# A convolution stage and a gated MLP on one core: absolute values, weight splits and a spectrum product moved between engines, and a new instruction order

## The chip, the cores and the metric

The kernel runs on one core of a Trainium2 chip. The metric is the device time of one execution in microseconds. The core's engines are named as in the profile: PE (TensorE, matmuls; PEld is its weight load), DVE (VectorE), ACT (ScalarE), POOL (GpSimd) and SP (SyncE, which issues most DMAs). Each engine works through its own list of instructions in order; semaphores between them carry the dependencies.

## The reference

A state-space convolution (S4D), and behind it a gated MLP (gMLP), each on a layer-normalized input and with a residual. L = 2048 positions, D = 512 channels, 128 states, all in float32.

```python
def A(u):                                   # S4D, as a long convolution
    dt = exp(log_dt)
    A = -exp(log_A_real) + 1j * A_imag;  C = (C_real + 1j * C_imag) * dt[:, None]
    P = exp((A * dt[:, None])[:, :, None] * arange(L))
    K = 2.0 * einsum("dn,dnl->dl", C, P).real
    y = irfft(rfft(u.T, 2 * L) * rfft(K, 2 * L))[..., :L].T
    return y + u * D_skip
def B(x):                                   # gMLP
    z = gelu(x @ w_in);  z1, z2 = z[..., :896], layernorm(z[..., 896:])
    g = einsum("ts,bsf->btf", w_sp, z2) + b_sp[None, :, None]
    return (z1 * g) @ w_out
h = x + A(layernorm(x));  out = h + B(layernorm(h))
```

## The kernel before, in words

**First phase (`phase_a`): the convolution as a Fourier transform by matmuls.** The channels are split in four stages, c = 0 to 3. Before the stages come the parameters (`params`, three calls: stage 0, stage 1, stages 2 and 3 together; absolute values and phases of C, phase increments split in a high and a low half, written to a stack in memory and loaded back as `sw`), the step sizes (`exp_exact`, a polynomial on 4 columns), tables of decays (`table`) and the layer norm of the input (`norm_x`, statistics on DVE, scaling on ACT and POOL).

The kernel K is built in 32 units of 16 channels (`unit`), eight to a stage. A unit's phases are two matmuls (`ps<-c_k,sw`); ACT takes sines and absolute values, POOL builds three decay tiles by products (`wa<-mt`) and weights one factor (`wb<-wb,wa`), DVE forms the factors (`f<-...`, `wa<-ps,wa`), and two groups of small matmuls (`ps<-f`, `ps<-wa,wb`) give `ks`. Then, by pieces:

- `piece_a` and `piece_c`, first step of the transform of the input and of K: 64x64 matmuls (`ps<-wb,...`).
- `piece_b`, second step for the input: 128x128 matmuls with 128 columns (`ps<-trio,a`, `ps<-big,a`), and `exchange`, a DMA that swaps halves of the spectrum between partitions.
- `piece_d`, second step for K (`ps<-big,a`), and at once the product with the input's spectrum in `trio` by DVE (`trio<-ps,trio`, 1024 elements). In stages 0 to 2 it works on the whole stage: eight groups of four matmul calls with 128 columns. In stage 3 it works in two halves of the channels: twice four groups of eight calls with 64 columns. Each call is two instructions in the trace.
- `piece_e`, the inverse transform (`ps<-c_inv,trio`), eight groups of 16 instructions a stage, copied to `big` by ACT or DVE.

All these calls are first recorded and then issued in an order written out by hand: `RANKS` gives every recorded call its place, `FORMS` chooses between two engines where the code offers two (`nc.either`), `BANKS` gives each result its PSUM bank. As all are issued from one helper, all have line L251. PSUM has five such banks here (three of double width).

**Between the phases.** Calls behind the last use of the units' buffers (the list is cut there) are issued by `rest`, inside the next phase, after that phase's loads (`xq`, `g`, `w1r`) have been put on SP's queue. After each of the last four copies of stage 3's `piece_e`, `rest` issues one quarter of the split of `w1` into a high and a low part (`split`: ACT casts, L688, and DVE subtracts, L689).

**Second phase (`phase_b1`).** `lines` finishes the inverse transform for a quarter n of the positions (`y<-big,g`, L754, four PSUM tiles), `add` adds the input, `moments` takes statistics (L780), `centre` and `root` the norm; `put_by` lets ACT copy a quarter's lines out of PSUM to a `stash` (L766), so that `add` later reads the stash (L771). For n = 0, `add` reads PSUM (L776) directly. The ACT table load for the next function (L893) stands ahead of the first lines. `column` is the first MLP product (`pz`, L880). Then follow the second half of that product (L982), the large product with `w_sp` (L1187) and the output (L1110).

Of the kernel before, what the change touches and what calls it, by code (L numbers as in the profile page):

```python
# [16 lines left out]
P = 128  # L17
# [20 lines left out]
    "0I000F0g1r0O0i0o0p1H1L1n1o0w2l1M2Z2L0805040302010607090A0B0C0D0E0G0H0K0N0R0T0Q0V0Y0X0J0x0y0z1E1G1T0L0U0S0a0k0l2i0+100-1B"  # L38
    "1F1J1P1Q1S1X1Y1d1q1y1t1u1v1w1z2J1611171h242P0M1W0c0Z0P1s0f180e270s2g2O2N1g0n0j1+2Q4a5F0h1l2A2Y3N121a0v0b1C0d1U0W14130r0t"
    "1f0m0q0u191A1Z151D1I1O1b1N1V1e1R1j1K1c1i252628292E2h2H2I2R2U2a2d2k2n2p2s2u2x2+312-3q3c3r373U3332393p363G3z3a383B3e3A644D"  # L40
    "3s4x453y443Q4u4J3f3b4X3H734K6t4L2F3O2w222T3S302K2f1x213F2y3C2V3I2C233J2B2r2m3P3E3W3R343M3L2e3K2o3X3Y3g3h3l3+3m3v3w3x3-41"
    "474A4E4G4Q4R4V4b4p514q525d5P4e726P6v4y5E4i6q4+5s534s6T5t4v4h5q4d4c6A5L4n546k624f4g5I4t5w7l7C768W8d1k1m2G2X2t3d3u481p1-20"
    "2D2M2bBd2j2q2z3Z3n3o494H4U4W4k4o5Q5u4O4P696B6C6D3T42434S6d6n4N4-675v6G6H6o6-775J5o5c6F6L6MHm6e6f6g6h6y6z70797A7B7I7J9K9f"
    "8UAY969UAZC3AdEk9c9-A0AlBBBGClFJFK6J6K6Q6R5N5O686E5S5V5y5-6N6O5k5r6m6u6p6w82837r7s7j7q7X7Z7a7b7V7W84852v3D3j4F4T4j4B4I4m"
    "4l564r575T6+7d7e2W2c2S353V3i3k3t46404Y4C4Z506I8T8b5G5H5K5U5W5X5Y5Z5a5b5n5j60666i7x7z4M4z5B4w5859555A5D5C5e5R5h5m8n9B9I7t"
    "7w7P7Y7c7k8E6S656X6U6V6W6Y6Z6a6b6s6c6x717+9F9L5M5l5i5x5z615f5g5+5p6j636l6r8B8e8f7T7m7g7R7S7U7Q7f7n7o7y7p87888Z97987L7O8A"
    "7K7M7N7u7v868C8J8D8S8i8s9495999x819C9R9Z9o898G787D7G7H8o8t8M8N7h7i74757E7F8w9DAqAr8u939k9l9J9YACAU9s9tAsAt9uABAMAc9N9jA8"
    "AG9g9nATAX9e9m9M9WBPBQCdCpCICQBiC8C9CABfBgCMCUCGCHCeE08H8X8O7-808F8K8Q8I8a8Y8P8j8k8r8vA9AgAh8L8g8m8R8V8c8q8l8y8p91909S92"
    "9a9b9+A+B09O8x9A8h8z8+9E8-9T9P9G9H9V9QA2A3B7BNBO9X9w9p9d9h9i9v9zA1ADA59qA6AEAFAPAQAmApBzBrBqBTBUBwBx9rAHAK9yA4A7ARAAAIAO"
    "AJANAVASAeAfCRDfDgAWAoALAaAbAiAyAnAjA-AuAkB6BABCBJBjDNDOB4AvBDB1B2B3BRBKBHBnBIBEBkBSBoC5D7DKDMBLBMBYB5BVBXBsBWBhBpBeBlBm"  # L50
    "BtBuC4CgD0D1CwCVDcBvCrDpDvAwAzAxB8B9BFBbBcC7BZBaCWCECOCFCXCYCbCZCkE5C+C-DWEHEIDUDtDSDeDDDPD5DEDXDZE2EAE8EGEpEtD+ECDzE3Dy"
    "E1EqEyD-EBEMEVETEZFtFuFZFbGTGaGIGbFAFLFpFvFkFlGSGVGUHGCBByC1B-C0CJCSCDCNCaCKCLCcCTCtCvEJFRFUCPC6CCB+C2CiCoCfCmD2CnCjCyCq"
    "D3DBDaF4F5CsD9D8ChCuCxCzDJD6DdDHDGDhDIDlDsFqH5HADLDRDAD4DCDFDVDjDQDkDTDYDiDbDnDxEXFSFTELEsDmFXDoFcFdDwENESEREYEgErEjElF0"
    "EiEhE-EvF9FDF-GhGoE4DrDqDuE6E9EUE7EDEKEEEFEcEWEmEnF7GNGcFYFPFGE+FEFVFsFFFiFjFeFrFyG1G2G6G7GgGnF2EzF6EwExF8FQFMFBFNFIFHFa"
    "FWFgFhG+G-H2FOF1HSHVFCHjHtEQEaEeEOEPEbEfEoFoEdEuF3FzG3GBF+GJGCGiGjGOGPHFHHI6I7GrGsGuGvHuHvHUHfHOHbHLHMHQHaHpHqHkHlHnHoHi"
    "H-HrHsHZHgHYHeIUIWIkIlIOIQIPIXIoIrIIIJImInILIMIpJPGWG5G4GDGEGFGeGQGXGYGRGdGyGfH6HBHzJFJGFxFwFnFfFmG0G9G8GAGGGLGKGZGMGlGm"
    "IyIzJ7GkHCHIH7HDHJHWHcHTHdHRHKHhHXHxHyIqJHJIGHGxGtGpGqGwH0H3H1H4GzH8H9HEHNHPItIuI-I3IKI1I4I5I9IbINIFIvIRIAIYIwIxJ1JaJcJd"
# [97 lines left out]
def exp_exact(nc, al, x, n):  # L155

    k, z, p = al(n), al(n), al(n)
    nc.vector.tensor_scalar(x, x, -87.0, 88.0, op0=ALU.max, op1=ALU.min)
# [7 lines left out]
    for i in range(7, 0, -1):
        nc.vector.scalar_tensor_tensor(p, p, co[i], z, op0=ALU.add, op1=ALU.mult)
    nc.vector.tensor_scalar(k.bitcast(I32), k, 127.0, 8388608.0, op0=ALU.add, op1=ALU.mult)
    nc.vector.scalar_tensor_tensor(x, p, 1.0, k, op0=ALU.add, op1=ALU.mult)
    return x  # L170
# [516 lines left out]
def split(nc, hi, lo, src):  # L687
    nc.scalar.copy(hi, src)  # L688
    nc.vector.tensor_sub(lo, src, hi.bitcast(F32))  # L689
# [8 lines left out]
def phase_b1(tc, es, right, left, rest, c_mean, mhalf, qt, ins, cst, wp, scr):  # L698
# [69 lines left out]
    def add(n, g):  # L768
        v = xqs[n % 3][:, 4 * g:4 * g + 4, :]
        if n:  # L770
            nc.vector.tensor_add(v, stash[n][:, g].rearrange("p (l x) -> p l x", l=4), v)  # L771
        else:
            h, y = g % 2, ys[n, g].rearrange("p l (x d) -> p l d x", d=4)
            v = xqs[n % 3][:, 4 * (g - h):4 * (g - h) + 8].rearrange("p l (d x) -> p l d x", d=4)[64 * h:64 * h + 64]
            for odd in range(2):
                nc.vector.tensor_add(v[:, odd::2], y[64 * odd:64 * odd + 64], v[:, odd::2])  # L776
# [523 lines left out]
```

## Time and profile before

| | |
|---|---|
| median of 3 runs | 854.41 us (850.94 to 854.44) |
| the profiled execution | 856.65 us; its span, first to last instruction, 854.9 us |
| granted PE clock, mean over the span | 0.972 of full speed |
| PE busy | 790.9 us (93%) |
| DVE, ACT, POOL busy | 612.4, 448.8, 286.7 us |

In the profile's rows, "128x64 f32 x16 [1.03 <-DVE big L251]" is 16 instructions on 128 partitions and 64 columns, ahead of which the engine was idle for 1.03 us until DVE's write to `big`. "Issue" is waiting for which the profile shows no cause. Durations of neighbours on one engine overlap slightly, since an instruction begins before the last one's end is noted. PE's granted clock is a share of full speed; where the clock is low, busy time is long time.

### The profile page before, as it was taken

Reading aid. Unit: us, or ns where it says so; the run is one execution under the profiler, and the core shown is the slowest. Engines: PE = TensorE matmul, PEld = TensorE weight load, DVE = VectorE, ACT = ScalarE, POOL = GpSimd, SP = SyncE. Lnnn points to the kernel's source line nnn. Section 1 sums busy time; section 2 is a strip of 40 time slices with the busy share of each in tenths; the row PEclk is TensorE's granted clock in tenths of the full one; section 3 lists DMA queues with packets and bytes.
Section 4 is the critical chain, followed back from the end, with each engine's and each line's share of the span. In section 5 each row is a group of like instructions: output and inputs, shape, how many; then the busy total and the mean of one; then the engine's idle time right before and its main releaser. Section 6 shows DMA issues by size and latency. Waiting matters only on the chain.

```text
span 854.9 us, 20107 instructions
## 1 busy us (share of the span) xinstructions
PE 790.9 (93%) x8145; PEld 674.4 (79%) x8145; DVE 612.4 (72%) x1176; ACT 448.8 (52%) x796; POOL 286.7 (34%) x340
## 2 busy tenths in 40 slices
PE   1569999999989877999999999999999999999998
PEld 0347789888978876788899988888888888888887
DVE  8999987777851357864357679988966985788533
ACT  6979988886740037555323255456534533354111
POOL 6969999976550000000032100224222002232200
PEclk9979999999995699999999999999999999999999
DMA  8504522525048113655246034899989547799632
GB/s 273 175 2 139 133 61 55 122 57 111 6 105 328 50 51 97 163 147 185 88 109 148 16 109 124 189 211 214 220 197 203 184 137 185 161 241 246 164 108 77
DMA packets 65005, 119.49 MB, mean 140 GB/s; under 512 B 6801, under 2 KB 21265, under 8 KB 63633
## 3 DMA queue, kind: packets, MB, share of 16 engines
q1 hardware_dynamic: 53248, 96.71, 38.2%
q0 software_dynamic: 11664, 21.50, 15.1%
q8 instruction: 64, 1.05, 0.5%
q14 instruction: 29, 0.23, 0.1%
HBM read 90.40 MB, written 19.40 MB: 128 GB/s over the span
## 4 chain that ended last, share of the span: by engine, by line
PE 84%; DVE 8%; ACT 5%; issue 2%; DMA 1%; SPq 0%; ACTq 0%; DVEq 0%
PE m L1187 33%; PE ps L251 25%; PE pz L982 9%; PE pz L880 7%; PE po L1110 7%; PE pl L1110 2%; DVE trio L251 2%; ACT big L251 2%; DVE f L251 1%; DVE ps L251 1%; DVE big L251 1%; DVE stats L780 1%; ACT ps L251 1%; DVE wa L251 1%; PE y L754 1%
## 5 line engine op out<-in xcount | busy, mean ns | idle before, releaser
L1187 PE MATMUL m<-wts,zc_wa 128*128 128x512 f32 x700 | 221.0, 395 | 0.0
L1187 PEld LDWEIGHTS m<-wts,zc_wa 128*128 128x128 f32 x700 | 131.7, 188 | 30.9
L1187 PE MATMUL m<-wts,zc_wb 128*128 128x512 f32 x350 | 138.0, 394 | 0.0
L1058 POOL DMA_DIRECT2D raws<-in_w_sp_dram x64 | 58.0, 995 | 214.7 <-DMA raws<-in_w_sp_dram 214.1
L251 POOL TENSOR_TENSOR wa<-mt 128x512 f32<-128x512 f32 x96 | 106.5, 1129 | 25.7 <-PE ps L251 19.8
L688 ACT CAST wts<-raws 128x512 fp32r<-128x512 f32 x112 | 69.1, 620 | 55.4 <-DMA raws<-in_w_sp_dram 25.7
L689 DVE TENSOR_TENSOR wts<-raws,wts 128x512 fp32r<-128x512 f32 x112 | 76.5, 685 | 17.0 <-ACT wts L688 16.9
L1187 PEld LDWEIGHTS m<-wts,zc_wb 128*128 128x128 f32 x350 | 65.8, 188 | 15.6
L251 PE MATMUL ps<-big,a 128*128 128x128 f32 (+1 forms) x512 | 74.6, 311 | 3.1 <-DVE big L251 1.0
L982 PE MATMUL pz<-w,ht 128*128 128x448 f32 x384 | 77.0, 362 | 0.0
L880 PE MATMUL pz<-ht,w1h 128*128 128x512 f32 (+1 forms) x248 | 73.8, 377 | 2.6 <-ACT ht L837 2.2
L251 PEld LDWEIGHTS ps<-big,a 128*128 128x128 f32 x512 | 71.0, 222 | 6.4 <-issue 1.3
L982 PEld LDWEIGHTS pz<-w,ht 128*128 128x128 f32 x384 | 72.0, 187 | 4.9
L988 POOL TENSOR_SCALAR sm<-sm 128x1 f32<-128x1 f32 x16 | 5.5, 344 | 209.3 <-DVE sm L987 209.3
L251 PE MATMUL ps<-c_inv,trio 128*128 128x128 f32 x512 | 65.6, 291 | 5.8 <-DVE big L251 3.2
L251 PEld LDWEIGHTS ps<-c_inv,trio 128*128 128x128 f32 x512 | 63.1, 205 | 7.4 <-DVE big L251 3.4
L1110 PE MATMUL po<-w,gz 128*128 128x512 f32 x252 | 61.7, 392 | 0.0
L251 DVE TENSOR_TENSOR trio<-ps,trio 128x1024 f32<-128x1024 f32 (+1 forms) x34 | 38.5, 1162 | 31.2 <-PE ps L251 27.5
L688 ACT CAST zc_wa<-raws 128x384 fp32r<-128x384 f32 (+1 forms) x70 | 36.9, 532 | 42.8 <-DVE raws L1092 22.4
L251 ACT COPY big<-ps 128x512 f32<-128x512 f32 x49 | 28.1, 588 | 58.1 <-PE ps L251 57.7
L1110 PEld LDWEIGHTS po<-w,gz 128*128 128x128 f32 x252 | 47.3, 188 | 10.7
L251 DVE TENSOR_TENSOR f<-ps,wa 128x512 f32<-128x512 f32 (+1 forms) x64 | 47.0, 750 | 11.7 <-ACT ps L251 9.8
(168 smaller groups left out, 1461.3 us busy)
## 6 DMA issues: line engine op xcount, KB each, us to landing
raws<-in_w_sp_dram SPq DMA_DIRECT2D x112, 256.0 KB, 4.1
raws<-in_w_sp_dram POOLq DMA_DIRECT2D x80, 256.0 KB, 5.9
trio<-trio SPq DMA_DIRECT2D x32, 256.0 KB, 4.4
scr_z<-zo SPq DMA_DIRECT2D x28, 256.0 KB, 2.1
big<-in_u_a_dram SPq DMA_DIRECT2D x8, 512.0 KB, 6.1
xq<-in_u_b_dram SPq DMA_DIRECT2D x4, 1024.0 KB, 8.8
g<-in_c_g_dram SPq DMA_DIRECT2D x4, 1024.0 KB, 7.7
scr_h<-xq SPq DMA_DIRECT2D x16, 256.0 KB, 4.3
```

The source lines that it names most:

```text
L251: r = getattr(getattr(self.nc, e), method)(*map(self.real, args), **{k: self.real(x) for k, x in kw.items()})
L688: nc.scalar.copy(hi, src)
L689: nc.vector.tensor_sub(lo, src, hi.bitcast(F32))
L754: nc.tensor.matmul(ys[n, g][o:o + 64, i, :], gs[n][w, l, r], qv[w, r, 16 * n + l], start=(r == 0), stop=(r == 1), tile_position=(64 * h, o))
L780: nc.vector.bn_stats(stats[:, n % 2, i, :], xqs[n % 3][:, i, :])
L880: nc.tensor.matmul(pt[:, w], a[:, q, f], ht[n][k][:, q, w], start=((q, i) == terms[0]), stop=((q, i) == terms[-1]))
L982: nc.tensor.matmul(pt[:, :FQ], a[:, q], w2[:, b, q, f], start=(q == 0 and i == 0), stop=(q == 3 and i == 2))
L988: nc.gpsimd.tensor_scalar_add(sm[:, 14:15], sm[:, 13:14], 1e-5)
L1058: nc.gpsimd.dma_start(r, ws[1], accum_op=ALU.add)
L1110: nc.tensor.matmul(pt, gz[fb][x][:, P * a:P * a + P], wo[:, y, fb, w], start=(first and fb == fbs[0] and i == 0), stop=(last and fb == fbs ...
L1187: nc.tensor.matmul(pt, x[:, f], y, start=(k == 0 and i == 0), stop=(k == KT - 1 and i == 2))
```

## The change

1. The parameters' six absolute values (`b` and `a` of three `params` calls) are ACT's `Abs` where DVE computed max(-x, x) of a tile in SBUF.
2. `exp_exact` keeps three of its tiles in PSUM, with one more instruction; the four `sw` memsets, the products `co`, `si`, the low halves and the weighting `wt` of the later units, which were DVE's or POOL's by `FORMS`, are POOL's.
3. `piece_d` of stage 3 is whole, as in the other stages. For its groups 1, 3 and 5 ACT copies the PSUM tile to SBUF and POOL does the product, in two instructions of 512 elements.
4. The four subtractions of the `w1` split are POOL's, and are issued after the second to fifth copies of stage 3's `piece_e` (by rank).
5. The first lines (n = 0) go through `put_by` and a stash too, like the others; the table load stands behind the copies of n = 0 and n = 1.
6. `RANKS`, `FORMS` and `BANKS` are new. The recorded calls go from 392 to 377 on DVE, 323 to 333 on ACT, 223 to 235 on POOL; PE keeps 280 groups and SP 70.

Read out by rank, PE's groups from unit 30's phases on are (U is a unit, with its two products; C, D, E the pieces of stage 3; `l` and `h` the halves):

```
before: U30 phases, U31 prod0, prod1, C0, C2, Dl3, C5, C7, U30 prod0, prod1, Dl2, C4, C6,
        Dh0, Dh3, Dh1, Dh2, Dl0, Dl1, E6, E7, E5, E2, E0, E4, E1, E3
after:  U30 phases, C2, U31 prod0, prod1, C5, U30 prod0, C0, U30 prod1, C6, C7, C4,
        D1, D4, D3, D2, D5, D7, D0, D6, E4, E1, E3, E6, E2, E5, E7, E0
```

DVE's products of Dl3, Dl2 and Dl0 stand behind E5 before. The last two exchange issues stand on either side of U30's phases before, and both ahead of them after. At the start, POOL has 13 instructions ahead of the last low half of the first stack before, and 18 after.

```diff
-def exp_exact(nc, al, x, n):
-    k, z, p = al(n), al(n), al(n)
+def exp_exact(nc, al, ps, x, n):
+    w, k, z, i = (al(n) for _ in range(4))
+    y, r, p = ps
...
-            nc.either(lambda: nc.vector.memset(sws[h][o:o + 32], 1.0), lambda: nc.gpsimd.memset(sws[h][o:o + 32], 1.0))
-    nc.vector.tensor_copy(dts, ldt)
-    exp_exact(nc, pm0, dts, NCH)
+            nc.gpsimd.memset(sws[h][o:o + 32], 1.0)
+    b = bank("dt", [P, 3, NCH])
+    e = exp_exact(nc, pm0, [b[:, i] for i in range(3)], ldt, NCH)
...
-        nc.vector.scalar_tensor_tensor(b, ci, -1.0, ci, op0=ALU.mult, op1=ALU.max)
+        nc.scalar.activation(b, ci, AF.Abs)
...
-        nc.vector.scalar_tensor_tensor(a, cr, -1.0, cr, op0=ALU.mult, op1=ALU.max)
+        nc.scalar.activation(a, cr, AF.Abs)
...
-            nc.either(lambda: nc.vector.tensor_sub(x, x, hi),
-                      lambda: nc.gpsimd.tensor_tensor(x, x, hi, op=ALU.subtract))
+            nc.gpsimd.tensor_tensor(x, x, hi, op=ALU.subtract)
...
-            nc.either(lambda: nc.gpsimd.tensor_tensor(wt, wt, mv[:, 2], op=ALU.mult), lambda: nc.vector.tensor_mul(wt, wt, mv[:, 2]))
+            nc.gpsimd.tensor_tensor(wt, wt, mv[:, 2], op=ALU.mult)
...
-    def piece_d(c, g, lo, n):
-        kn = 1 << (P // n).bit_length() - 1
-        pt = bank("s2", [P, 2 * n, 2 * kn])
+    def piece_d(c, g):
+        pt = bank("s2", [P, 64, 8])
         with nc.group():
-            for j in range(kn):
...
+            for j in range(4):
...
-        nc.vector.tensor_mul(v, pt.unsqueeze(1).to_broadcast([P, 2, 2 * n, 2 * kn]), v)
+        if c + 1 == NCH and g in (1, 3, 5):
+            t = trio[:, 0, 512 * (g // 2):512 * (g // 2) + 512].rearrange("p (x m) -> p x m", m=8)
+            nc.scalar.copy(t, pt)
+            for i in range(2):
+                nc.gpsimd.tensor_tensor(v[:, i], t, v[:, i], op=ALU.mult)
+        else:
+            nc.vector.tensor_mul(v, pt.unsqueeze(1).to_broadcast([P, 2, 64, 8]), v)
...
-        for lo, n in ((0, 32),) if c + 1 < NCH else ((0, 16), (16, 16)):
-            for g in range(n // 4):
-                piece_d(c, g, lo, n)
+        for g in range(8):
+            piece_d(c, g)
...
+        then = sorted(last, key=lambda o: o["rank"])[1:5]
...
-                if o in last:
+                if o in then:
                     next(between)
...
-def split(nc, hi, lo, src):
+def split(nc, hi, lo, src, engine=None):
     nc.scalar.copy(hi, src)
-    nc.vector.tensor_sub(lo, src, hi.bitcast(F32))
+    (engine or nc.vector).tensor_tensor(lo, src, hi.bitcast(F32), op=ALU.subtract)
...
-    rest(split(nc, w1h[:, q], w1l[:, q], w1r[:, q]) for q in range(4))
+    rest(split(nc, w1h[:, q], w1l[:, q], w1r[:, q], nc.gpsimd) for q in range(4))
...
-    stash = {n: hp.tile(...) for n, t in ((1, "h20"), (2, "h30"), (3, "h31"))}
+    stash = {n: hp.tile(...) for n, t in ((0, "h10"), (1, "h20"), (2, "h30"), (3, "h31"))}
...
-        nc.scalar.activation(stats[:, 1, 0, 0:1], mhalf, AF.Gelu_apprx_tanh)
         for n in range(2):
             for g in range(0, 4, 2):
                 lines(n, g, g + 1)
-        for g in range(0, 4, 2):
-            for f in add, moments:
-                f(0, g)
-                f(0, g + 1)
+        for n in range(2):
+            for g in range(4):
+                put_by(n, g)
+        nc.scalar.activation(stats[:, 1, 0, 0:1], mhalf, AF.Gelu_apprx_tanh)
         for g in range(4):
-            put_by(1, g)
+            add(0, g)
+            moments(0, g)
         centre(0)
```

More of the change, by code (lines that the diff above doesn't have):

```diff
@@ L37 @@
 RANKS = (
[L38 to L57, printed above, removed]
@@ L69 @@
-    "30023400301040213320243121044330112"
+    "414220313014444030432220022044434342124120412142014001422000123112321121011031223434430243400423134324420430131103321432"
+    "034214411300222000123324434132420203334344321432242224410132113203001432002102101211314313432104023143234243141003422442"
+    "030104322301034014314303413333144024"
 )
@@ L152, in rsqrt @@
     return y
-def exp_exact(nc, al, x, n):
-    k, z, p = al(n), al(n), al(n)
-    nc.vector.tensor_scalar(x, x, -87.0, 88.0, op0=ALU.max, op1=ALU.min)
-    nc.vector.tensor_scalar(k, x, 1.0 / math.log(2.0), MAGIC, op0=ALU.mult, op1=ALU.add)
-    nc.vector.tensor_scalar(k, k, MAGIC, None, op0=ALU.subtract)
+def exp_exact(nc, al, ps, x, n):
+    w, k, z, i = (al(n) for _ in range(4))
+    y, r, p = ps
+    nc.vector.tensor_scalar(y, x, -87.0, 88.0, op0=ALU.max, op1=ALU.min)
+    nc.vector.tensor_scalar(k, y, 1.0 / math.log(2.0), MAGIC, op0=ALU.mult, op1=ALU.add)
+    nc.vector.tensor_scalar(r, k, MAGIC, None, op0=ALU.subtract)
+    nc.vector.tensor_copy(w, y)
     hi = 0.693359375
-    nc.vector.scalar_tensor_tensor(z, k, -hi, x, op0=ALU.mult, op1=ALU.add)
-    nc.vector.scalar_tensor_tensor(z, k, hi - math.log(2.0), z, op0=ALU.mult, op1=ALU.add)
+    nc.vector.scalar_tensor_tensor(z, r, -hi, w, op0=ALU.mult, op1=ALU.add)
+    nc.vector.scalar_tensor_tensor(z, r, hi - math.log(2.0), z, op0=ALU.mult, op1=ALU.add)
     co = [1.0 / math.factorial(i) for i in range(9)]
     nc.vector.tensor_scalar_mul(p, z, co[8])
[L166 to L170, printed above, removed]
+    for d in range(7, 0, -1):
+        nc.vector.scalar_tensor_tensor(p, p, co[d], z, op0=ALU.add, op1=ALU.mult)
+    nc.vector.tensor_scalar(i.bitcast(I32), r, 127.0, 8388608.0, op0=ALU.add, op1=ALU.mult)
+    nc.vector.scalar_tensor_tensor(p, p, 1.0, i, op0=ALU.add, op1=ALU.mult)
+    return p
 class Late:
@@ L460, in params @@
                 nc.sync.dma_start(stk_d[c0 + c, h].rearrange("r p n -> p r n"), st6[64 * h:64 * h + 64, :, c, :])
-        times(co, co, mx, ALU.mult)
-        times(si, si, mn, ALU.mult)
-        times(co, co, si, ALU.add)
+        nc.gpsimd.tensor_tensor(co, co, mx, op=ALU.mult)
+        nc.gpsimd.tensor_tensor(si, si, mn, op=ALU.mult)
+        nc.gpsimd.tensor_tensor(co, co, si, op=ALU.add)
         for c in range(n):
@@ L621, in piece_e @@
         e = evac(o, pt.rearrange("p d r -> p r d"))
-        if c + 1 == NCH and s >= 4:
+        if c + 1 == NCH:
             last.append(e)
@@ L759, in phase_b1 @@
         load_g(n)
-    stash = {n: hp.tile([P, 4, 512], F32, tag=t, name=f"stash{n}") for n, t in ((1, "h20"), (2, "h30"), (3, "h31"))}
+    stash = {n: hp.tile([P, 4, 512], F32, tag=t, name=f"stash{n}") for n, t in ((0, "h10"), (1, "h20"), (2, "h30"), (3, "h31"))}
     def put_by(n, g):
@@ L769, in add @@
         v = xqs[n % 3][:, 4 * g:4 * g + 4, :]
[L770 to L776, printed above, removed]
+        nc.vector.tensor_add(v, stash[n][:, g].rearrange("p (l x) -> p l x", l=4), v)
     def moments(n, g):
```

44 lines of the change are left out of this document (30 added, 14 removed).

## Prediction

> **What bounds the kernel now.** I read the page's totals, then the busy time by stretches of the span (columns: PE, PEld, DVE, ACT, POOL busy us and instructions, granted clock, DMA share, GB/s), then PE's timeline where that table shows loss.
>
> ```profile
> span 854.9 us, 20107 instructions
> PE 790.9 (93%) x8145; PEld 674.4 (79%) x8145; DVE 612.4 (72%) x1176; ACT 448.8 (52%) x796; POOL 286.7 (34%) x340
> PEclk9979999999995699999999999999999999999999
> ...
> 0.00:40.00 40.00, 11.91 (x57) 7.22 (x61) 37.44 (x153) 31.43 (x70) 31.31 (x43) 1.00 0.73 239
> 40.00:60.00 20.00, 14.08 (x348) 9.88 (x340) 18.97 (x21) 14.93 (x34) 13.35 (x15) 0.74 0.01 3
> 60.00:240.00 180.00, 173.16 (x4196) 154.65 (x4187) 144.87 (x196) 151.46 (x216) 148.94 (x158) 1.00 0.34 81
> 240.00:265.00 25.00, 19.75 (x491) 17.93 (x490) 10.08 (x14) 9.99 (x18) 9.66 (x15) 0.86 0.76 228
> 265.00:286.00 21.00, 20.75 (x97) 20.75 (x98) 4.90 (x4) 0.19 (x1) 0.00 (x0) 0.50 0.42 169
> 286.00:313.00 27.00, 19.69 (x135) 19.15 (x139) 9.88 (x11) 6.38 (x10) 0.00 (x0) 0.82 0.15 44
> 313.00:345.00 32.00, 25.60 (x592) 23.89 (x587) 25.12 (x76) 21.32 (x39) 0.00 (x0) 1.00 0.41 109
> 345.00:855.00 510.00, 505.96 (x2265) 420.92 (x2265) 361.18 (x705) 213.09 (x414) 83.44 (x112) 1.00 0.64 159
> ```
>
> PE is the bound from 60 to 240 us (173.16 of 180) and from 345 us on (505.96 of 510). The diff touches nothing behind 345 us, so what is won ahead of it comes off the end one for one. Ahead of it lie three losses: the first 60 us, where DVE is the full engine (37.44 of 40 and 18.97 of 20); the last stage, 240 to 313 us; and the first lines, 313 to 345 us. The last stage hides its loss from the busy share: from 265 to 286 us PE is busy 20.75 of 21.00, at a granted clock of 0.50. PE's timeline there:
>
> ```profile
> 227.54 1.05 PE L251 MATMUL ps<-big,a 128*128 128x128 f32 x8
> ...
> 238.95 5.62 PE L251 MATMUL ps<-c_inv,trio 128*128 128x128 f32 x48
> ...
> 246.36 0.73 PE L251 MATMUL ps<-c_k,sw 128*128 128x512 f32 x2
> ...
> 251.73 1.97 PE L251 MATMUL ps<-big,a 128*128 128x64 f32 x16 [1.03 <-DVE big L251]
> ...
> 254.72 0.32 PE L251 MATMUL ps<-f 128*32 128x64 f32 x8
> 257.65 0.54 PE L251 MATMUL ps<-f 128*32 128x64 f32 x24 [2.60 <-issue]
> ...
> 258.95 3.68 PE L251 MATMUL ps<-big,a 128*128 128x64 f32 x16
> ...
> 265.25 20.75 PE L251 MATMUL ps<-big,a 128*128 128x64 f32 x96 [0.70 <-ACT big L251]
> 285.79 7.02 PE L251 MATMUL ps<-c_inv,trio 128*128 128x128 f32 x48
> 295.37 7.25 PE L251 MATMUL ps<-c_inv,trio 128*128 128x128 f32 x48 [2.56 <-DVE trio L251]
> 305.87 5.46 PE L251 MATMUL ps<-c_inv,trio 128*128 128x128 f32 x32 [3.24 <-DVE big L251]
> 312.82 4.37 PE L754 MATMUL y<-big,g 64*64 64x128 f32 x148 [1.50 <-ACT w1h L688]
> ```
>
> The rows with 128x64 are the last stage's piece_d in halves, 128 matmuls in 1.97 + 3.68 + 20.75 = 26.4 us. Warm, one takes 1.97 / 16 = 123 ns; under the 0.50 clock 20.75 / 96 = 216 ns. An earlier stage's piece_d, whole, takes 1.05 / 8 = 131 ns for a matmul of twice the columns. A matmul here costs nearly the same with 64 columns as with 128, and whole there are 64 of them.
>
> ```profile
> 284.00:288.00 4.00, 4.00 (x20) 4.00 (x20) 1.22 (x1) 0.00 (x0) 0.00 (x0) 0.50 0.27 51
> 288.00:292.00 4.00, 4.00 (x35) 4.00 (x34) 1.17 (x2) 1.42 (x2) 0.00 (x0) 0.90 0.54 215
> ```
>
> The clock comes back about 3 us after piece_e's 128x128 matmuls begin (285.79), while 20 us of unbroken 128x64 matmuls hadn't brought it back. Whole piece_d has piece_e's shape. [...]
>
> **The last stage, part by part.** I count from unit 30's phase matmuls (246.36), ahead of which both rank tables put the same 253 groups of PE work, to the first lines (312.82): 66.5 us now.
> - Up to the second half of piece_d: 265.25 - 246.36 = 18.9 us. The new order has no piece_d in this stretch: less 1.97 + 3.68 leaves 13.2. I keep the 2.60 us in which PE waits for nothing shown.
> - Piece_d: 64 x 131 ns = 8.4, plus 1.5 for a cold start of some 3 us at 216 instead of 123 ns: 9.9. With all of it at 216 ns, 13.8.
> - Hand-over: all eight products must be in trio before piece_e. The last one on DVE and the pair on POOL come in below: 1.5.
>
> ```profile
> 291.84 3.48 DVE L251 TENSOR_TENSOR trio<-ps,trio 128x1024 f32<-128x1024 f32 x3
> 304.12 1.09 DVE L689 TENSOR_TENSOR w1l<-w1r,w1h 128x896 fp32r<-128x896 f32 x1 [8.80 <-ACT w1h L688]
> ...
> 289.31 0.58 ACT L251 COPY big<-ps 128x512 f32<-128x512 f32 x1 [24.12 <-PE ps L251]
> ...
> L251 POOL TENSOR_TENSOR wa<-mt 128x512 f32<-128x512 f32 x96 | 106.5, 1129 | 25.7 <-PE ps L251 19.8
> ```
>
> DVE's product is 3.48 / 3 = 1.16 us, so the last group costs about that. The three groups that go to ACT and POOL cost ACT 3 x 0.58 and POOL 6 x 1.13 = 6.8, beside the 8.4 of PE; the last POOL pair belongs to the fifth of eight groups and ends about level. Five products of 1.16 keep DVE ahead of PE, where eight (9.3) would not.
> - Piece_e: 8 x 5.62 / 3 = 15.0 warm, where 25.5 go by now (285.79 to 311.33), with 2.56 lost behind products left for late and 3.24 behind a split and copies. The four DVE splits of 1.09 are gone; on POOL I estimate 896 / 512 x 1.13 = 2.0 each, 8 in all, on an engine that does 0.00 there, done before the lines. Then 0.7 for the last copy, where 1.50 stand.
>
> 13.2 + 9.9 + 1.5 + 15.0 + 0.7 = 40.3, a gain of 26.2; I take 25, keeping 1.2 for the w1 casts among ACT's copies. On SP the last exchange now stands ahead of unit 30's phases, so the next phase's loads, w1 among them, start no later than now. Ends: 14 (piece_d all cold, 3.9 more; piece_e's 19.7 as now, 4.7 more; one bubble of 3.24) and 30 (no 2.60 gap, no cold start).
>
> **The first 60 us.** The DVE timeline, POOL's beside it, and the chain that ended last:
>
> ```profile
> 17.07 2.66 DVE L251 SCALAR_TENSOR_TENSOR ps<-trio 128x128 f32<-128x128 f32 x1
> ...
> 44.85 4.08 DVE L251 SCALAR_TENSOR_TENSOR big<-big 128x256 f32<-128x256 f32 x1
> ...
> 52.31 0.42 DVE L251 SCALAR_TENSOR_TENSOR ps<-big 128x256 f32<-128x256 f32 x1
> ...
> 44.27 4.37 POOL L251 TENSOR_TENSOR wa<-mt 128x512 f32<-128x512 f32 x4
> ...
> 17.15 2.58 DVE ps L251
> ...
> 46.38 2.47 issue
> ...
> 26.38 1.19 PE L251 MATMUL ps<-c_k,sw 128*128 128x512 f32 x2 [3.43 <-DMA sw<-scr_stk]
> ```
>
> Two of the six absolute values took 2.66 and 4.08 us; the form takes 0.42 at 256 columns. The longer one ended when four POOL products beside it had run back to back (48.6). The excess, 2.3 + 3.7 = 6.0, stands on the chain as 2.58 and the "issue" of 2.47, some 4.8 together. ACT gets the six at about 0.4 (it is busy 31.43 of 40, then 14.93 of 20), POOL two memsets, three weight products and one more product. Against it: the new order puts the first stack's low halves behind five more POOL instructions, and the first phase matmul already waits 3.43 for that stack. The exponential is one instruction of four columns longer, and SP issues the first input block one place later; both lie within these bounds. I take 3.5, with ends 8 (all the excess and DVE's memsets) and -3 (the stack as late as its wait is long, the absolute values hidden anyway).
>
> [...]
>
> **The dense part, 60 to 240 us.** PE idles 6.8 there, which bounds a gain. The new table wants POOL earlier: up to the weight products of units 14 and 15 it has 135 POOL instructions to 128, up to 30 and 31, 228 to 221, at like PE work; 7 x 1.13 = 8 us, against 31 that POOL idles in these 180. I take a loss of 1.5; ends -8 and +6.8.
>
> **The first lines.** DVE and ACT, and the matmul that waits for them:
>
> ```profile
> 314.82 2.83 DVE L776 TENSOR_TENSOR xq<-y,xq 64x512 f32<-64x512 f32 x4 [0.92 <-PE y L754]
> 317.69 1.65 DVE L780 BATCH_NORM_STATS2 stats<-xq 128x6 f32<-128x128 f32 x8
> ...
> 319.32 4.75 ACT L766 COPY stash<-y 64x512 f32<-64x512 f32 x8 [5.03 <-PE y L754]
> ...
> 323.90 0.62 PE L789 MATMUL lnh_pm<-stats,c_mean 128*128 128x16 f32 x4 [2.69 <-DVE stats L780]
> ```
>
> Now two rounds of 2.83 + 1.65 stand between 314.82 and the matmul at 323.90. Then ACT copies at 4.75 / 8 = 0.59, two for a group, and DVE follows with one add (2.83 / 4 = 0.71) and four statistics (0.82): 314.8 + 1.2 + 4 x 1.53 = 322.1, 1.8 earlier. ACT's sixteen copies end at 314.8 + 9.5 = 324.3, where the second lines' copies end now (324.1); the table load behind them meets no one until the third lines. Ends +2.7 (the halved adds) and -1 (that load).
>
> **Sum.** 3.5 - 1.5 + 25 + 1.8 = 28.8. The profiled execution took 856.65 (span 854.9): 827.9. It lies 2.2 above the median shown, 854.41, from which the sum gives 825.6. I take 827.
>
> **Rivals.**
> 1. Piece_d stays cold though whole. For it: 20 us at 0.50 with PE full. Against: the same shape in piece_e warms up. Then 13.8 for 9.9, and piece_e's first 3 us cold, 1.7 more: 833. [...]
> 2. The tail gains its lower end, 14, as gaps move into piece_e and the 2.60 grows (all loads of the next phase start here; DMA share 0.76): 838.
> 3. The dense part loses its 8 to POOL, or the absolute values were hidden: 834.
> 4. The first phase gains its 8 and the dense part loses nothing: 821; with some of the dense idle too, 819.
> 5. Slower than before: the clock falls inside the dense part, where the skinny shapes (128x64 and 64x64) may not bring it back, as in the last stage, where 26.4 us did what 128 x 123 ns = 15.7 does: 11 lost a spell. One leaves a gain, two (849) little of it, and from three on it is slower (860). For it: 0.74 at 40 to 60 us, with PE busy 14.08 of 20. Against: 1.00 over all of 60 to 240.
>
> **How the numbers follow.** My forecast 0.40; rival 1, 0.15; 2, 0.13; 3, 0.12; 4, 0.12; 5 with two spells 0.04, with three or more 0.04. Half a percent, 4.3 us, is about what can be told from no change here: faster 0.92, same 0.04, slower 0.04. 816 to 843 leaves out rival 5 and the far ends of 2 and 4; my forecast's own range is 821 to 832.
>
> **What would show it.** Last stage: 64 matmuls of 128x128 from big and a in 8 to 10 us at a clock of 1.00 for most of it; eight inverse groups in about 15 with no gap over 1.5; lines some 40 us behind unit 30's phases. First 60 us: no DVE instruction of 2.6 or 4 us, and the dense part reached 3 to 4 us sooner. PE idle from there to unit 30 under 10. The statistics' matmul 9 to 7 us behind the first lines. It fails if the clock stays at 0.50 through piece_d, or if PE shows new gaps on POOL's products.

## The result

The changed kernel took 820.43 us (median of 4 runs, 819.86 to 821.16), the kernel before 854.42 (4 runs beside them, 850.94 to 855.40): a ratio of 0.961, 95% interval 0.9582 to 0.9638. The two profiled executions took 856.65 and 819.86 us with spans of 854.9 and 818.1, so the traces have to account for 36.8 us, 2.8 more than the medians differ by. The old kernel's time varies with its clock: 19 further runs of it, beside the second group of experiments, spread from 837.30 us at a granted clock of 0.988 to 859.19 at 0.974, where the changed kernel's four all stand at 0.992, so the 34 us hold for its usual executions, and about 17 for its few fastest.

The page's totals after, and then the busy time by stretches (columns as in the prediction; cuts at unit 30's phases, 235.20, and at the first lines, 274.87):

```profile
span 818.1 us, 20010 instructions
PE 766.9 (94%) x8081; PEld 652.2 (80%) x8081; DVE 592.3 (72%) x1153; ACT 456.3 (56%) x813; POOL 308.5 (38%) x356
PEclk9999999999998999999999999999999999999999
```

```profile
0.00:40.00 40.00, 12.99 (x94) 8.63 (x95) 35.12 (x152) 35.58 (x83) 36.25 (x47) 1.00 0.73 239
40.00:60.00 20.00, 16.17 (x531) 11.43 (x534) 18.77 (x23) 20.00 (x41) 19.92 (x25) 1.00 0.03 6
60.00:235.20 175.20, 171.78 (x4101) 154.95 (x4090) 138.33 (x184) 147.11 (x213) 147.18 (x155) 1.00 0.34 86
235.20:274.87 39.67, 33.13 (x514) 30.94 (x514) 17.11 (x22) 12.81 (x19) 21.42 (x19) 0.87 0.71 249
274.87:286.00 11.13, 7.93 (x260) 7.45 (x260) 5.95 (x20) 8.73 (x16) 0.00 (x0) 1.00 0.32 105
286.00:289.40 3.40, 3.40 (x62) 3.36 (x65) 1.29 (x5) 2.04 (x3) 0.00 (x0) 0.50 0.99 189
```

Of the kernel before, the stretch from 60 us to the same phases:

```profile
60.00:246.36 186.36, 179.52 (x4332) 160.65 (x4322) 148.49 (x202) 155.57 (x223) 154.97 (x167) 1.00 0.34 82
```

PE's timeline after, from unit 30's phases on:

```profile
235.20 0.73 PE L252 MATMUL ps<-c_k,sw 128*128 128x512 f32 x2
...
241.03 0.65 PE L252 MATMUL ps<-f 128*32 128x64 f32 x32 [1.75 <-DVE f L252]
...
248.20 8.24 PE L252 MATMUL ps<-big,a 128*128 128x128 f32 x56 [0.70 <-ACT big L252]
256.94 1.16 PE L252 MATMUL ps<-big,a 128*128 128x128 f32 x8 [0.49 <-DVE trio L252]
259.50 14.65 PE L252 MATMUL ps<-c_inv,trio 128*128 128x128 f32 x128 [1.41 <-DVE trio L252]
274.87 7.57 PE L756 MATMUL y<-big,g 64*64 64x128 f32 x256 [0.72 <-ACT big L252]
285.55 0.68 PE L785 MATMUL lnh_pm<-stats,c_mean 128*128 128x16 f32 x4 [3.11 <-DVE stats L776]
286.15 5.28 PE L756 MATMUL y<-big,g 64*64 64x128 f32 x128
```

The 36.8 us, by the places at which both traces can be cut:

| stretch | before | after | difference |
|---|---|---|---|
| start to unit 30's phases | 246.36 | 235.20 | -11.2 |
| to the first lines | 66.46 | 39.67 | -26.8 |
| to the statistics matmul (`lnh_pm`) | 11.08 | 10.68 | -0.4 |
| to the end of the span | 531.0 | 532.55 | +1.55 |

The last stage gave what was predicted. The part ahead of it gave 9 us more, and behind the first lines something was lost that the prediction has no term for: PE waits 3.11 us, the clock is 0.50 for the 3.4 us behind the wait, and the second lines take 5.28 us.

### The profile page after: what moved, and what is told of

Same layout as the page of the kernel before. It is cut to its first block, busy times and chain, and to the rows that moved or that the text cites. A ratio compares the mean times of both kernels' runs of the same rounds, so it can differ in the third digit from the quotient of the medians.

```text
span 818.1 us, 20010 instructions
## 1 busy us (share of the span) xinstructions
PE 766.9 (94%) x8081; PEld 652.2 (80%) x8081; DVE 592.3 (72%) x1153; ACT 456.3 (56%) x813; POOL 308.5 (38%) x356
## 4 chain that ended last, share of the span: by engine, by line
PE 61%; DVE 1%; ACT 1%; issue 0%
PE m L1183 34%; PE pz L978 9%; PE pz L876 8%; PE po L1106 7%; PE pl L1106 2%; DVE stats L776 0%; ACT ht L833 0%; ACT w1r L824 0%; DVE w1r L831 0%; DVE xq L772 0%; ACT stash L768 0%; DVE ht L837 0%; PE lnh_pm L785 0%; PE lnh_pv L799 0%; ACT zo L879 0%
## 5 line engine op out<-in xcount | busy, mean ns | idle before, releaser
L690 ACT CAST wts<-raws 128x512 fp32r<-128x512 f32 x112 | 69.1, 619 | 51.3 <-PE m L1183 26.2
L252 PE MATMUL ps<-c_inv,trio 128*128 128x128 f32 x512 | 60.8, 277 | 1.9 <-DVE trio L252 1.4
L252 PEld LDWEIGHTS ps<-c_inv,trio 128*128 128x128 f32 x512 | 58.5, 192 | 3.3 <-POOL trio L252 1.6
L252 PE MATMUL ps<-big,a 128*128 128x128 f32 x448 | 57.4, 285 | 1.2 <-ACT big L252 0.7
L252 PEld LDWEIGHTS ps<-big,a 128*128 128x128 f32 x448 | 53.8, 197 | 3.7 <-DVE trio L252 0.9
L876 PEld LDWEIGHTS pz<-ht,w1h 128*128 128x128 f32 x248 | 45.1, 188 | 12.8 <-ACT ht L833 3.5
L690 ACT CAST zc_wa<-z 128x128 fp32r<-128x128 f32 (+2 forms) x56 | 23.7, 431 | 45.6 <-PE m L1183 38.7
```

The costliest lines, as they stand in the source:

```text
L252: r = getattr(getattr(self.nc, e), method)(*map(self.real, args), **{k: self.real(x) for k, x in kw.items()})
L876: nc.tensor.matmul(pt[:, w], a[:, q, f], ht[n][k][:, q, w], start=((q, i) == terms[0]), stop=((q, i) == terms[-1]))
```

## The experiments

Twelve kernels, in three groups, each run together with the kernel before. Its medians differ between the groups (854.20, 853.34 and 852.15), and the changed kernel itself was not run in them. So a difference of two or three us from its 820.43 is told by the profiles, one for each kernel, and not by the medians; in the second group I compare the kernels of the group with each other.

### Where the first 11 us come from: the absolute values

Theory P: VectorE's absolute values cost the start what they last beyond 0.4 us, and GpSimd's products beside them are what draws them out (in the kernel before the one of 2.66 us ends at 19.73 and GpSimd's run of products at 19.57, the one of 4.08 at 48.93 and the products at 48.64). Theory O: the new order makes the early gain. The changed kernel with only this undone (`c1_abs_dve`), and the kernel before with only this done, the same edit the other way round (`c2_abs_act`):

```diff
-        nc.scalar.activation(b, ci, AF.Abs)
+        nc.vector.scalar_tensor_tensor(b, ci, -1.0, ci, op0=ALU.mult, op1=ALU.max)
...
-        nc.scalar.activation(a, cr, AF.Abs)
+        nc.vector.scalar_tensor_tensor(a, cr, -1.0, cr, op0=ALU.mult, op1=ALU.max)
```

> The kernel after, with the six absolute values back on VectorE as max(-x, x) of two SBUF inputs, at their new places in the order. Theory P (these instructions were shut out by GpSimd's products, and that is most of what the first 60 us won): some of the six last 1.5 to 4 us again, and the time is 824 to 828 us. Theory O (the first phase won by the new order and the other moves; the long instructions had cover): 819 to 822 us.

Measured: 822.26 us (819.99 to 826.08), ratio 0.964; unit 30's phases at 237.53. VectorE's rows:

```profile
15.27 0.61 DVE L252 SCALAR_TENSOR_TENSOR ps<-trio 128x128 f32<-128x128 f32 x1 [0.45 <-DMA trio<-in_par_dram]
...
34.75 0.57 DVE L252 SCALAR_TENSOR_TENSOR big<-big 128x256 f32<-128x256 f32 x1
...
46.96 1.21 DVE L252 SCALAR_TENSOR_TENSOR ps<-big 128x256 f32<-128x256 f32 x1
```

> The kernel before, with only the six absolute values moved to ScalarE, at their old places in the order. Theory P: the rows of 2.66 and 4.08 us go, the norm's last addition comes 4 to 6 us sooner, and the time is 848 to 850 us. Theory O: the rows go, but ScalarE is late with its copies instead, and the time is 853 to 855 us.

Measured: 847.79 us (840.74 to 850.23, 10 runs), ratio 0.9928, interval 0.9887 to 0.9968. In its profile the last addition of the input's norm starts at 43.27 (48.85 before, 41.92 after), unit 30's phases at 238.32, and the clock is 1.00 from 40 to 60 us where it was 0.74:

```profile
43.27 1.19 DVE L251 TENSOR_TENSOR big<-big,ps 128x1024 f32<-128x1024 f32 x1
...
40.00:60.00 20.00, 15.71 (x529) 10.99 (x528) 18.76 (x24) 20.00 (x45) 18.27 (x24) 1.00 0.10 22
```

So the single edit brings 8.0 of the 11.2 us in the old order, and undoing it costs only 2.3 in the new one, where the same instructions take 0.57 to 1.21 us instead of 2.66 and 4.08. These are the phases of one profile each: by the medians the edit brings 6.4 us in the old order (854.20 to 847.79), and the 2.3 can't be told. Each theory holds in one order: either edit removes most of the same loss. Why these instructions are shorter in the new order was not tried (the one of 1.21 us, from 46.96, has a product of GpSimd beside it from 46.78 to 47.87), and that the products lengthen them was not shown: no run took the products away.

### The last stage: shape, order or clock

The changed kernel with all eight products of the last stage on VectorE (`c3_dve8`):

```diff
-        if c + 1 == NCH and g in (1, 3, 5):
...
-        else:
-            nc.vector.tensor_mul(v, pt.unsqueeze(1).to_broadcast([P, 2, 64, 8]), v)
+        nc.vector.tensor_mul(v, pt.unsqueeze(1).to_broadcast([P, 2, 64, 8]), v)
```

> The kernel after, with all eight products of the last stage on VectorE (no copy by ScalarE, none on GpSimd). If the sharing matters: eight products of 1.16 us take 9.3 us beside 8.4 us of warm matmuls, the inverse transform starts 1 to 2.5 us later, 821.5 to 823 us. If the cold start gives VectorE its time anyway, the gap ahead of the inverse transform stays at 1.4 us: 820 to 821 us.

Measured: 823.72 us (821.63 to 825.91), ratio 0.9666, interval 0.9609 to 0.9724: the medians don't tell it from the changed kernel. By the profile it is 42.0 us from unit 30's phases to the first lines instead of 39.67, with these rows:

```profile
257.04 1.16 PE L252 MATMUL ps<-big,a 128*128 128x128 f32 x8 [1.10 <-DVE trio L252]
260.44 17.11 PE L252 MATMUL ps<-c_inv,trio 128*128 128x128 f32 x128 [2.23 <-DVE trio L252]
```

PE waits 0.6 and 0.8 us longer for `trio`, and behind that the clock is 0.50 (258.99 to 265.82), which makes piece_e 2.5 us longer: the clock costs more than the waits. As the clock falls at other places than in the changed kernel's profile, what the sharing alone is worth stays open.

Then the same with piece_d in halves again (`c4_halves`), all 128 of its matmuls of 128x64 behind the last piece_c:

```diff
...
-        for g in range(8):
-            piece_d(c, g)
+        for lo, n in ((0, 32),) if c + 1 < NCH else ((0, 16), (16, 16)):
+            for g in range(n // 4):
+                piece_d(c, g, lo, n)
```

Theory S: the 128x64 shape itself runs at the low clock. Theory T: the shape only costs its own time, and the order sets the clock, which in the changed kernel is back 3.4 us behind the wait for the statistics (0.50 from 286.00 to 289.40 with PE busy throughout).

> As c3_dve8, but the last stage's piece_d in halves of the channels again, 128 matmuls of 64 columns for 64 of 128, all behind the last piece_c. Theory S (the clock is kept low by the 128x64 shape, however busy PE is): 0.50 through all of piece_d, 27 us of it, and into piece_e: 837 to 842 us. Theory T (any unbroken work brings the clock back within some 3.4 us; in the kernel before something else held it down): a cold start as in the kernel after, then 123 ns a matmul, 16 to 17 us of piece_d: 827 to 829 us.

Measured: 822.88 us (822.32 to 828.29), ratio 0.967, no slower than the whole piece_d beside it.

```profile
247.89 14.51 PE L252 MATMUL ps<-big,a 128*128 128x64 f32 x128
264.18 14.56 PE L252 MATMUL ps<-c_inv,trio 128*128 128x128 f32 x128 [1.79 <-DVE trio L252]
```

```profile
247.89:262.40 14.51, 14.50 (x133) 14.36 (x128) 7.69 (x7) 2.72 (x5) 1.11 (x1) 1.00 1.01 415
```

128 of them in 14.51 us, 113 ns each, at a clock of 1.00: theory S falls. (In `c3_dve8` the eight whole groups took until 258.2, 9.5 us; but then PE waits for VectorE there, and not here. From unit 30's phases to the first lines it is 42.0 and 43.2 us.) Yet 96 of these matmuls ran at 0.50 to the end in the kernel before, 20.75 us. The theory that fits both, S2: piece_d's 128x64 matmuls keep a full clock, but don't bring a low one back, and 128x128 matmuls do. Its rival T2: the shape has no part in it, and the clock follows what else goes on there. The first test (`e5_before_warm`) was the kernel before with 28 unused 128x128 instructions, 14 matmul calls, between its last piece_c and the second half of its piece_d:

```diff
+            for j in range(14):
+                nc.tensor.matmul(pt, a2v[:, j, :], a2v[:, j + 1, :].rearrange("p (a b) -> p a b", b=2), start=True, stop=True)
...
+    junk(14)
```

> The kernel before, with fourteen matmul calls (28 instructions) of 128x128 on constants added ahead of the second half of piece_d; their result is not used. Theory S2 (at a low clock the 128x64 shape can't bring the clock back, at full clock it keeps it; 128x128 does bring it back): the added work takes 5 to 7 us, the clock is back before it ends, the 96 instructions behind it take 11 to 12 us instead of 20.75, and the time is 849 to 852 us. Theory T2 (something else holds the clock down in that stretch, such as the loads that fill the DMA engines until 274 us, and it ends by itself): 0.50 stays through piece_d and the added work comes on top, 859 to 861 us.

Measured: 848.68 us (840.26 to 853.75, 10 runs), not to be told from the kernel before (interval of the ratio 0.9922 to 1.0102). In the profiled run the clock had not fallen at all ahead of them: the wait for nothing shown was 1.13 us this time, not 2.60, and stands further on.

```profile
257.40 0.38 PE L251 MATMUL ps<-wb,ks 64*64 64x64 f32 x9 [1.13 <-issue]
257.71 3.39 PE L251 MATMUL ps<-a 128*128 128x128 f32 x28
260.94 10.83 PE L251 MATMUL ps<-big,a 128*128 128x64 f32 x96
271.61 5.58 PE L251 MATMUL ps<-c_inv,trio 128*128 128x128 f32 x48
```

So it is no test of a recovery; it shows that the old order's own 96 matmuls take 10.83 us, not 20.75, once the clock is full at their start. From unit 30's phases (244.35) to the first lines (297.21) this run took 52.86 us, some 49.5 without the unused matmuls. So about 17 of the 66.5 us are the low clock, and the other 10 of the last stage's 26.8 us are gained against the old order at full clock too. The clean test makes PE idle ahead of piece_d (17.22 and 21.52 us, as it came out), once with halves (`c4_halves` with the delay: `e6_halves_idle`) and once whole (`c3_dve8` with it: `e7_whole_idle`), with the same delay: nine copies of 1024 elements on ScalarE ahead of the last copy that piece_d needs. A window, in the two expectations, is 3.4 us long, like the stretch of 286.00 to 289.40 at 0.50 in the changed kernel, and "one busy window whatever the shape" is theory T.

```diff
+        for i in range(9):
+            nc.scalar.copy(trio[:, 0, 0:1024], trio[:, 0, 1024:2048])
```

> As c4_halves (128 instructions of 128x64, which there ran at full clock), with nine copies of 1024 elements put ahead of ScalarE's copy of the last piece_c, so that PE stands idle for 8 to 9 us ahead of piece_d and must begin at a low clock. Theory S2: piece_d stays at 0.50 for its whole length, 27 us instead of 14.5, and the inverse transform starts cold too: 844 to 848 us. Theory T2 or one busy window whatever the shape: one or two cold windows, piece_d 16 to 18 us, 832 to 836 us.

> As c3_dve8 (64 instructions of 128x128), with the same nine copies. Theory S2 and theory T2 both: the clock is back within one or two windows of piece_d, which takes 10 to 13 us, 832 to 836 us. Should both shapes stay cold, 840 us and more.

Measured: 855.22 us (853.58 to 855.50) with halves, 843.68 (842.55 to 844.43, 10 runs) whole. The delay was about twice what I had estimated, as casts of `w1` stand between the copies in ScalarE's list and the first of them waits for its load (7.72 and 9.02 us). So both lie 7 to 12 us above what S2 expected, but their difference, 11.5, is the answer. With halves, PE's rows and the stretch of its piece_d; then the same whole, its stretch cut where the clock rises:

```profile
267.28 24.15 PE L252 MATMUL ps<-big,a 128*128 128x64 f32 x112 [17.22 <-ACT big L252]
292.75 16.39 PE L252 MATMUL ps<-c_inv,trio 128*128 128x128 f32 x128 [1.32 <-DVE trio L252]
```

```profile
267.28:291.50 24.22, 24.15 (x112) 23.96 (x112) 7.20 (x7) 0.05 (x1) 6.26 (x3) 0.50 0.00 0
```

```profile
267.77 8.16 PE L252 MATMUL ps<-big,a 128*128 128x128 f32 x56 [21.52 <-ACT big L252]
```

```profile
267.77:271.14 3.37, 3.37 (x16) 3.37 (x16) 1.23 (x1) 0.05 (x1) 3.19 (x2) 0.50 0.02 5
271.14:276.00 4.86, 4.79 (x42) 4.60 (x41) 3.64 (x4) 0.00 (x0) 3.11 (x2) 1.00 0.00 0
```

Halves: 24.15 us at 0.50, 216 ns each, PE without a gap and the DMA engines idle; the clock rises only in piece_e (0.50 over 252 to 296 us, 0.98 over 296 to 312). Whole: it is back after 3.37 us. Without the delay the two kernels took the same time (822.88 and 823.72 us). S2 is shown for these matmuls, whose weights are 128x128 (the 128*128 of a row).

The 64 columns alone are not the reason. In `c3_dve8` the clock is 0.50 for 3.4 us (241.93 to 245.33) ahead of piece_d; all the work there has 64 columns behind smaller weights, and the clock is back behind it:

```profile
242.29 1.08 PE L252 MATMUL ps<-f 128*32 128x64 f32 x32 [1.75 <-DVE f L252]
243.30 1.13 PE L252 MATMUL ps<-wb,ks 64*64 64x64 f32 x32
244.36 1.08 PE L252 MATMUL ps<-wa,wb 128*32 128x64 f32 x32
...
242.29:245.30 3.01, 3.01 (x96) 2.62 (x96) 1.23 (x1) 0.76 (x2) 0.00 (x0) 0.50 0.94 200
245.44:246.34 0.90, 0.00 (x1) 0.00 (x0) 0.76 (x2) 0.18 (x1) 0.21 (x1) 1.00 0.99 196
```

In `e6_halves_idle` the clock rose at 248.8, ahead of the long wait: behind 2.84 us of 64x64 and 1.4 us into piece_d's halves (0.72 over 240 to 252 us). What in the shape decides was not tried. At either clock a matmul of piece_d takes about as long with 64 columns as with 128 (216 and 211 ns at 0.50, 113 and 118 at 1.00), with the weight load busy throughout (PEld 23.96 of 24.22 us). So the load may set the pace with either shape: my estimate from these numbers, not shown.

Last, 22 unused 128x128 instructions (`c8_warm`; 6, 3 and 2 calls like those of `e5_before_warm`) in three gaps ahead of piece_d of the changed kernel, whose clock was 0.50 from 241.60 to 251.84:

```profile
241.60:251.84 10.24, 8.63 (x185) 8.08 (x178) 2.42 (x4) 2.83 (x5) 1.02 (x2) 0.50 1.00 326
```

> The kernel after, with 22 matmul instructions of 128x128 on constants, results unused, put into three places where PE waits between unit 30's phases and piece_d (12, 6 and 4). If idle windows there are what costs the clock: 1.00 through unit 30 and piece_d, the ten cold us go, and the time is 816.5 to 818.5 us. If the added work stands in the way of the chain, or the clock falls all the same: 820 to 822 us.

Measured: 823.03 us (819.51 to 826.15), ratio 0.9762, interval 0.963 to 0.9895, beside widely spread runs of the kernel before. In its profile the clock is full through piece_d (56 instructions in 6.51 us, not 8.24), but PE has a new wait for nothing shown of 1.70 us and the unused work to do. From unit 30's phases to the first lines it is 38.84 us instead of 39.67: no gain that the runs can tell. The dip itself comes and goes: the profiles of `c6_lines_psum` and the three kernels behind it, below, have the same code there, the same wait of 1.75 us and no dip. Of `c6_lines_psum`, from unit 30's phases to the first lines:

```profile
246.53 6.61 PE L252 MATMUL ps<-big,a 128*128 128x128 f32 x56 [0.73 <-ACT big L252]
...
235.26:271.56 36.30, 29.57 (x514) 27.51 (x514) 17.12 (x22) 12.63 (x20) 21.46 (x19) 1.00 0.78 272
```

36.30 us instead of 39.67, with the 56 instructions of piece_d in 6.61.

### The first lines

The first lines of the changed kernel added from PSUM by VectorE again (`c6_lines_psum`):

```diff
-        nc.vector.tensor_add(v, stash[n][:, g].rearrange("p (l x) -> p l x", l=4), v)
+        if n:
+            nc.vector.tensor_add(v, stash[n][:, g].rearrange("p (l x) -> p l x", l=4), v)
+        else:
...
+            for odd in range(2):
+                nc.vector.tensor_add(v[:, odd::2], y[64 * odd:64 * odd + 64], v[:, odd::2])
```

> The changed kernel with its first lines added from PSUM by VectorE again, in the old order, and the stash without its first quarter; everything else is as changed. Theory of the prediction: the copies by ScalarE save time, so without them the statistics matmul comes 1.8 us later behind the first lines: 822 to 823 us. Theory of the traces (one add of the changed kernel waits for the copies of two groups, four of them, and while it waits TensorE idles 3.11 us and then runs lines(2) at half clock): the way from the first lines to the statistics matmul is the old 11.1 us instead of 10.7, but TensorE's idle time ahead of the statistics stays near the 1.5 us of the kernel before, lines(2) takes 3.7 us instead of 5.3, and the time is 819 to 820.5 us.

Measured: 818.02 us (816.54 to 821.27), ratio 0.9608. The statistics matmul comes 11.09 us behind the first lines, as expected, but PE waits 3.45 us ahead of it, not 1.5, and the second lines take 5.37: that half of my expectation was wrong, and the wait is not the new copies' doing.

The low halves of `w1` on VectorE again (`c7_split_dve`):

```diff
-    rest(split(nc, w1h[:, q], w1l[:, q], w1r[:, q], nc.gpsimd) for q in range(4))
+    rest(split(nc, w1h[:, q], w1l[:, q], w1r[:, q]) for q in range(4))
```

> The changed kernel with the low halves of w1 subtracted by VectorE again instead of GpSimd. If the subtractions are hidden there too (VectorE has 15 us of piece_e with some 16 copies that it keeps ahead of): 820 to 821 us. If the subtractions, 1.1 us each by the trace of the kernel before, hold back the products' way to the first lines, TensorE waits 1 to 3 us inside piece_e or ahead of the first lines, and its clock may fall behind the wait: 822 to 825 us.

Measured: 818.57 us (818.31 to 821.45), ratio 0.9617, no difference that these runs can tell. By the profile piece_e and the hand-over to the first lines take 16.70 us, against 15.36 in `c6_lines_psum` (256.20 to 271.56), with these waits:

```profile
270.36 2.05 PE L252 MATMUL ps<-c_inv,trio 128*128 128x128 f32 x16 [0.60 <-DVE big L252]
273.60 7.22 PE L756 MATMUL y<-big,g 64*64 64x128 f32 x256 [1.20 <-ACT big L252]
```

Eight unused 128x128 matmuls in the wait ahead of the statistics (`c9_junk`):

```diff
+        for _ in range(8):
+            nc.tensor.matmul(jk[:, 0:P], c_mean, c_mean, start=True, stop=True)
         centre(0)
```

> The changed kernel with eight 128x128 matmuls (16 instructions, results unused) on TensorE ahead of the statistics matmul, in the 3.11 us in which it idles. If the half clock behind that wait (285.98 to 289.39 us of the changed kernel's profile) is what costs: the clock stays at 1.00 there, lines(2) takes 3.7 us instead of 5.3, and the time is 818.5 to 819.5 us. If ScalarE and VectorE set the pace of these stages: 820 to 821 us, with the 1.6 us turned into a wait ahead of the next matmuls.

Measured: 818.68 us (815.39 to 820.21), ratio 0.9605. In the profile the wait is 0.88, the clock stays full, and the second lines take 3.72 us:

```profile
279.55 2.05 PE L901 MATMUL warm<-c_mean 128*128 128x128 f32 x16
282.48 0.59 PE L785 MATMUL lnh_pm<-stats,c_mean 128*128 128x16 f32 x4 [0.88 <-DVE stats L776]
283.00 3.72 PE L756 MATMUL y<-big,g 64*64 64x128 f32 x128
```

From the statistics matmul to the end it is 531.1 us instead of 532.55: the 1.5 us of the half clock come through to the end in the profile; the medians can't tell it. The last kernel, `c9_lines`, has the same eight matmuls, and shares the first lines: groups 0 and 1 added from PSUM while ScalarE copies groups 2 and 3, with the table load ahead of the lines again (here against `c6_lines_psum`).

```diff
...
-        if n:
+        if n or g >= 2:
             nc.vector.tensor_add(v, stash[n][:, g].rearrange("p (l x) -> p l x", l=4), v)
...
```

> The changed kernel with the first lines mixed: groups 0 and 1 added from PSUM by VectorE, groups 2 and 3 by way of ScalarE's copies, the table load ahead of the lines, and the same eight matmuls ahead of the statistics. If the pair-wise copies are why the change gave 0.4 us here and not 1.8: the statistics matmul comes about 9.7 us behind the first lines instead of 10.7, lines(2) runs at full clock, and the time is 817.5 to 819 us. If ScalarE's copies for the later groups only move back: 820 to 821 us.

Measured: 815.25 us (814.32 to 817.67), ratio 0.9578, interval 0.9544 to 0.9613: the lowest of all. Its runs lie below the changed kernel's, but so does the kernel before in this group, by 2.3 us, and the intervals of the two ratios overlap by a little (0.9582 to 0.9638 for the changed kernel), so the size of the gain is told by the profiles: 9.68 us from the first lines to the statistics matmul instead of 10.68, and 530.97 behind it.

## Why the prediction was right, step by step

The time fell as forecast and by more: 820.43 lies 0.6 us below the forecast's own 821 to 832, and is the time of rival 4, to which I gave 0.12. The largest term came out, in part by luck; the early terms were too small, and two late ones were wrong.

**Last stage: 25 taken, 26.2 worked out, 26.8 measured.** To piece_d 13.0 us (13.2 predicted); piece_d to its end 9.9 (9.9, with the cold start of 1.5: 56 instructions in 8.24 where 6.61 is warm); hand-over 1.41 (1.5); piece_e 14.65 (15.0); last copy 0.72 (0.7). Rivals 1 and 2 did not come, nor did rival 5: the clock is 1.00 from 60 to 235.20 us, and the skinny shapes that it feared bring a low one back in 3.4 us in `c3_dve8`. Two of the parts are right by luck. The 2.60 us wait that I kept in the 13.0 is not there; waits of 1.75 us for VectorE and 0.90 for GpSimd are, and a low clock, without which the same way takes 11.3 us (`c6_lines_psum`). And 131 ns for a warm matmul was too much (118), and a wait of 0.49 us ahead of the last group made up most of that. What the prediction could not see is how little the whole shape is worth where the clock is full when piece_d begins: 1.2 us between `c4_halves` and `c3_dve8` by the profiles (3.7 without the low clock in the latter's piece_e). In the changed kernel's profile it began low, and the whole shape brought it back in 3.6 us, as the prediction says. Halves in the new order made 43.2 us of the old 66.5, at full clock.

**First 60 us and dense part: 2.0 predicted, 11.2 measured.** These are the mis-sized terms. By 60 us PE had done 625 instructions (94 + 531), where 405 stood before, and PE's idle time from there to unit 30's phases fell from 6.84 to 3.42. So the dense part gained 3.4 where I took a loss of 1.5 (that term had the wrong sign: POOL is busy 147.18 of 175.20 there and has the room), and the first 60 us gained the other 7.7, near the end of 8 that I gave as the bound and not near the 3.5 that I took. I had priced 4.8 on the chain and then cut it for the longer way to the first stack; the first phases did come later (27.57 instead of 26.38), but this did not eat the gain. And I had left out the clock: the 0.74 from 40 to 60 us went with the absolute values alone (`c2_abs_act`). Rival 4 came, while the forecast's own last stage came too.

**First lines: 1.8 predicted, 0.4 measured.** My sum puts the matmul 9.3 us behind the first lines, my sign said 9 to 7, and it came at 10.68. The failed step is "ACT copies two for a group, and DVE follows". `put_by` writes the halves of a pair of groups, so the first add needs the copies of two groups. ACT's and DVE's timelines after:

```profile
277.00 9.55 ACT L768 COPY stash<-y 64x512 f32<-64x512 f32 x16 [2.18 <-PE y L756]
```

```profile
279.40 0.69 DVE L772 TENSOR_TENSOR xq<-stash,xq 128x512 f32<-128x512 f32 x1 [5.65 <-ACT stash L768]
280.13 0.87 DVE L776 BATCH_NORM_STATS2 stats<-xq 128x6 f32<-128x128 f32 x4
```

Copies from 277.00, four of 0.60 us, then four times 1.5: 285.5, where the matmul starts at 285.55. `c9_lines`, which needs no copy for its first two groups, gets the microsecond back.

**Behind the statistics: nothing predicted, 1.55 lost.** A wait of PE that I took for its own length costs half the clock behind it as well: 3.11 us here, 3.45 and 3.46 in `c6_lines_psum` and `c7_split_dve`, each with the second lines at 5.3 to 5.4 us; 1.47 in `c4_halves` and 0.88 in `c9_junk`, with 3.73 and 3.72. The length alone does not decide: 2.59 us in `c8_warm` was followed by second lines of 5.39, 2.69 in the kernel before by 3.72.

**Splits of `w1`: hidden on POOL, as predicted** (POOL's four take 260.24 to 268.86, 8.35 us, where I had 8); on DVE they cost 1.3 us in the profile, much less than the 3.24 that stood behind them before.

## What to carry to other kernels

Read the granted clock of a stretch before its busy share: here over 20 us at 0.50 with PE busy throughout were the largest single loss, with a gap of 2.60 us ahead of them. Where a gap can't be closed, let the matmuls behind it be of a shape that brings the clock back (here 128x128 in 3.37 us, where 24.15 us of 128x64 had not), or fill it with unused ones of that shape: by the profiles that paid 1.5 us ahead of the statistics and under 1 us ahead of piece_d. When a copy feeds an add, look which instructions write the piece that the add reads; and where two edits each remove the same loss, they do not add up (by the profiles the absolute values gave 8.0 us in the old order, and undoing them cost 2.3 in the new).

## What the runs showed of the hardware that was not expected

- Matmuls of 128x64 in float32 behind weights of 128x128 keep a full clock (113 ns each, 14.51 us at 1.00) and don't bring a low one back (216 ns each, 24.15 us at 0.50 with PE full and DMA at 0.00). Those of 128x128 bring it back in 3.4 us, and cost 118 ns (56 in 6.61 us). Those with 64 columns behind smaller weights (128*32 and 64*64) bring it back too, in 3.4 us in `c3_dve8`.
- Behind the same wait of 1.75 us ahead of the last products the clock fell in five profiles (the changed kernel, `c1_abs_dve`, `c3_dve8`, `c4_halves`, `e6_halves_idle`) and not in five others (`e7_whole_idle` and the four of the last group). The stretches at 0.50 of 3.40 (286.00 to 289.40 in the changed kernel), 6.83 (258.99 to 265.82 in `c3_dve8`) and 10.24 us (241.60 to 251.84 in the changed kernel) are about one, two and three times 3.4. What decides between the executions was not tried.
